# Reordered first loads and a tile of ones for the junk products, in a linear-attention and MLP-mixer kernel

## The chip, the cores and the metric

The kernel runs on one core of a Trainium2 chip. The core has five engines, each with its own instruction queue: TensorE (PE, matrix products; its weight loads are shown as PEld), VectorE (DVE), ScalarE (ACT), GpSimd (POOL) and SyncE (SP), which issues most of the transfers between device memory and on-chip memory. Sixteen transfer engines (DMA) carry them; loads that SP issues go into one set of queues, those that ACT issues into another. The metric is the device time of one execution in microseconds (us); less is better. Before the change it is 771.73 us, the median of three runs (771.15 to 772.42).

## The reference

Two blocks follow one another, in float32, with batch 8, 8 heads, 576 tokens and head size 64 (8 x 64 = 512 channels):

```python
kv  = einsum('bhsd,bhse->bhde', k, v)          # per head 64 x 64, summed over the 576 tokens
out = einsum('bhsd,bhde->bhse', q, kv)
x   = out / sqrt(mean(out * out, -1) + 1e-6) * g_norm   # then heads side by side: 576 x 512 per batch
h   = relu(x.T @ w_tok1) @ w_tok2              # 576 -> 256 -> 576, over tokens
u   = x + h.T
out = u + relu(u @ w_ch1) @ w_ch2              # 512 -> 1536 -> 512, over channels
```

The weights of the second block arrive as 64-bit floats and are turned into 32-bit ones on the chip.

## The kernel before

The batch is worked on in pairs. For each pair the attention runs first, then the mixing over tokens, and, after all pairs, the mixing over channels, which takes about two thirds of the time. The change touches only the first microseconds.

Of each batch's 576 tokens the first 512 are loaded as four rows of products (J = 4), the last 64 as a fifth. `load(b)` (line 141) brings k and v of batch b: for each a large transfer of 1 MB into `k_in[:, :4]` or `v_in[:, :4]`, and two small ones of 64 KB each, 32 token rows apiece, into the fifth row (j = 4). The other half of the fifth row's 128 partitions is zeroed by POOL (line 1286). For batch 0, k goes through SP's queue and v through ACT's; for later batches everything goes through SP's. `load_q(b)` (line 152) brings the transposed q (1 MB for 512 tokens). `get_tok1` (line 216) fetches the first token weights as raw 64-bit words into `raw`; ACT and DVE then turn them into `w_tok1` in four steps (lines 166 to 190).

The order in which the first loads are written is: `load(0)` (k, v and their small loads), `load_q(0)`, two blocks of `w_tok1`, `load(1)`, `load_q(1)`, the 64 last tokens of q for both batches, the last block of `w_tok1`; later in the text comes `g_norm` (`g_row`, one row of 256 bytes, on ACT's queue). Each engine keeps this order of its own instructions.

The order of the computing work is written out by hand as a list of short names, `start` (line 1304). Its first line begins with `j12`: `keep_warm(12)` (line 1341), twelve products of the identity with itself, whose result nobody reads. Then `kv00` and `kv01`, the products of k and v of batch 0 (`ps_kv`, 80 passes; a float32 product is two passes), each followed by `e00`, `e01`, a copy to `kvp`; `gs`, `spread_g` (line 1298), which spreads `g_row` to all 128 partitions by a product with a row of ones (`ps_g`) and a copy to `g_sb`; then `a00` to `a11`, the products with q (`ps_o`, 8 passes each); on DVE and ACT the factor g, the squares, their sums and the scaling; the steps `w01` to `w04`, the conversion of the first token weights; `j8`, eight more junk products; and `h000`, `h010`, the first products with them (`ps_h`). `kv10` is the `ps_kv` of batch 1.

For `kv00`, the products of j = 0 to 3 of the first half of the columns come first and need only the large loads; the next one, j = 4, reads the fifth row and so needs all four small loads:

```python
for i in range(2):
    for j in range(JJ):
        for h in range(2):
            matmul(o[...], lhsT=kk[:, j, at], rhs=vv[:, j, at], start=(j == 0), stop=(j == JJ - 1))
```

The semaphores between engines and transfers are set by the compiler layer. In the trace each load that SP or ACT issues takes one of eight counters in turn, and a load whose counter is still in use waits for the load that has it.

## Time and profile before

| what | value |
| --- | --- |
| median of the runs | 771.73 us |
| the profiled execution, time / span | 771.12 / 769.3 us |
| granted clock of PE | 0.999 |
| PE busy | 759.4 us, 99% of the span |
| DVE, ACT, POOL busy | 642.5, 277.4, 112.3 us |
| first junk product on PE | 3.34 us |
| first `ps_kv` product, and the restart after a wait | 8.81 and 9.82 us |
| first `ps_o` | 12.19 us |
| `ps_kv` of batch 1 | 21.67 us |

The span runs from the first instruction to the last; the execution's time has 1.8 us more around it. The profile lists groups of instructions with an engine, a line of the code, the tile that is written and those that are read. "Busy" is the time in which an engine worked on such instructions; behind it stand the idle time before a group and what ended that idle time. In the table of windows the columns are the stretch, its length, busy time and instructions of PE, PEld, DVE, ACT and POOL, the granted clock, the mean busy share of the transfer engines, and GB/s. `w_tok<-raw`, `x<-ps_o,g_sb` and the like read "written from".

### The profile page before, as it was taken

To read this page: it belongs to the slowest core of one execution; us is meant where nothing else is said; L and a number is where in the kernel's file an instruction comes from. 1 tells how busy PE (TensorE), PEld (TensorE's weight loads), DVE (VectorE), ACT (ScalarE), POOL (GpSimd) and SP (SyncE) were. 2 spreads that over 40 slices of the span, in tenths; PEclk is the share of its full clock that TensorE was granted. 3 is DMA by queue.
4 is the path that set the end of the run, shared out by engine and by line. 5 is a ranking of instruction groups with operands and counts; after the bars stand their busy time and mean duration, and the time that the engine had idled before them with its cause. 6 is when DMAs were issued, how large, how long until landed. Compare 5 with 4: busy or idle time off the path is not lost.

```text
span 769.3 us, 12678 instructions
## 1 busy us (share of the span) xinstructions
PE 759.4 (99%) x4676; PEld 612.3 (80%) x4676; DVE 642.5 (84%) x945; ACT 277.4 (36%) x556; POOL 112.3 (15%) x125
## 2 busy tenths in 40 slices
PE   7999999999999999999999999999999999999998
PEld 6665555445888888888888888888888888888887
DVE  3868897997767779899969889987998996798996
ACT  3555575764210233511244242123352223325221
POOL 1003020213410000002240001042000218000204
PEclk9999999999999999999999999999999999999999
DMA  9999998499699786589998577999659879955679
GB/s 339 366 366 370 373 372 301 151 318 342 251 286 339 271 282 191 164 270 207 216 236 251 158 224 216 255 188 267 202 148 290 172 220 208 207 145 157 151 200 119
DMA packets 137677, 188.26 MB, mean 245 GB/s; under 512 B 48658, under 2 KB 95250, under 8 KB 135570
## 3 DMA queue, kind: packets, MB, share of 16 engines
q1 hardware_dynamic: 101744, 167.54, 68.9%
q0 software_dynamic: 34816, 18.36, 16.1%
q10 hardware_dynamic: 1058, 1.57, 0.6%
q8 instruction: 37, 0.61, 0.3%
q14 instruction: 22, 0.18, 0.1%
HBM read 138.28 MB, written 49.15 MB: 244 GB/s over the span
## 4 chain that ended last, share of the span: by engine, by line
PE 97%; DMA 2%; SPq 0%; issue 0%; DVE 0%
PE ps_d L136 28%; PE ps_b L136 19%; PE ps_a L136 19%; PE ps_u L136 8%; PE ps_h L136 8%; PE ps_v L136 5%; PE ps_c L136 3%; DMA v_in<-in_v_dram 2%; PE ps_kv L136 2%; PE ps_o L136 2%; PE ps_w L136 2%; SPq L124 0%; PE ps_r L136 0%; DVE xs L127 0%
## 5 line engine op out<-in xcount | busy, mean ns | idle before, releaser
L136 PE MATMUL ps_d<-ui,w 128*128 128x256 f32 x504 | 118.6, 379 | 0.0
L136 PEld LDWEIGHTS ps_d<-ui,w 128*128 128x128 f32 x504 | 95.9, 190 | 12.9
L133 ACT COPY ps_d<-ps_a 128x768 f32<-128x768 f32 (+1 forms) x56 | 32.0, 572 | 200.2 <-PE ps_a L136 197.2
L127 DVE TENSOR_TENSOR v<-v,v 128x1536 f32<-128x1536 f32 (+2 forms) x70 | 103.2, 1482 | 0.3
L136 PE MATMUL ps_b<-sv,w 128*128 128x256 f32 x324 | 78.9, 380 | 0.0
L136 PE MATMUL ps_a<-v,w 128*128 128x256 f32 x324 | 78.8, 379 | 0.0
L1206 POOL DMA_DIRECT2D out_dram<-us x24 | 26.7, 1833 | 291.8 <-ACT p L133 286.2
L136 PEld LDWEIGHTS ps_b<-sv,w 128*128 128x128 f32 x324 | 61.3, 190 | 8.8 <-issue 0.6
L136 PEld LDWEIGHTS ps_a<-v,w 128*128 128x128 f32 x324 | 61.7, 190 | 8.2
L136 PE MATMUL ps_u<-h,w_tok 128*128 128x512 f32 (+1 forms) x160 | 64.7, 599 | 0.0
L136 PE MATMUL ps_d<-v,w 128*128 128x256 f32 x258 | 62.7, 379 | 0.0
L130 ACT ACTIVATE v<-v 128x768 f32<-128x768 f32 (+1 forms) x54 | 42.6, 822 | 55.1 <-DVE v L127 52.3
L136 PE MATMUL ps_h<-x,w_tok 128*128 128x512 f32 x128 | 57.8, 600 | 0.7 <-DVE w_tok L190 0.7
L1206 POOL DMA_DIRECT2D out_dram<-r x40 | 41.3, 1927 | 102.0 <-ACT p L133 80.3
L136 PE MATMUL ps_d<-sv,w 128*128 128x256 f32 x228 | 55.4, 379 | 0.0
L136 PEld LDWEIGHTS ps_d<-v,w 128*128 128x128 f32 x258 | 49.0, 190 | 6.5
L136 PEld LDWEIGHTS ps_u<-h,w_tok 128*128 128x128 f32 (+1 forms) x160 | 25.6, 179 | 31.1 <-issue 26.7
L136 PEld LDWEIGHTS ps_d<-sv,w 128*128 128x128 f32 x228 | 43.4, 190 | 5.8
L136 PE MATMUL ps_a<-uT,w 128*128 128x256 f32 x192 | 46.7, 379 | 0.0
L136 PEld LDWEIGHTS ps_h<-x,w_tok 128*128 128x128 f32 x128 | 23.4, 190 | 27.1 <-issue 24.1
L136 PE MATMUL ps_b<-ui,w 128*128 128x256 f32 x168 | 40.8, 379 | 0.0
L136 PEld LDWEIGHTS ps_a<-uT,w 128*128 128x128 f32 x192 | 36.5, 190 | 4.9
(169 smaller groups left out, 1288.0 us busy)
## 6 DMA issues: line engine op xcount, KB each, us to landing
w<-parts SPq DMA_DIRECT2D x168, 384.0 KB
w<-parts SPq DMA_DIRECT2D x56, 192.0 KB
uT<-blocks SPq DMA_DIRECT2D x36, 256.0 KB
k_in<-in_k_dram SPq DMA_DIRECT2D x8, 1024.0 KB
qT<-in_q_dram SPq DMA_DIRECT2D x8, 1024.0 KB
out_dram<-x POOLq DMA_DIRECT2D x16, 512.0 KB, 7.0
v_in<-in_v_dram SPq DMA_DIRECT2D x7, 1024.0 KB
raw<-in_moe_w_ch_dram SPq DMA_DIRECT2D x8, 768.0 KB
```

Source lines behind the costliest of these rows:

```text
L127: keep(engine.tensor_tensor(out=o, in0=a, in1=b, op=op))
L130: keep(nc.scalar.activation(o, a, AF.Relu))
L133: keep(nc.scalar.copy(o, a))
L136: keep(nc.tensor.matmul(*a, **kw))
L1206: keep(nc.gpsimd.dma_start(to, t()[ds(b * Q, Q), at].rearrange("p n l j -> p n (l j)"), accum_op=ALU.add))
```

## The change

The change has three parts. In `load(0)`, k's and v's large loads are issued as before (SP and ACT), then q of batch 0 on SP's queue, and then all four small loads on ACT's queue; later batches load as before. The text of the load of g is as it was, and comes later on ACT's queue. The junk products now multiply a 128 x 128 tile of ones, which DVE writes ahead of its other clears; the identity, which POOL made, is gone, and so is POOL's row of ones: `spread_g` uses the first row of the tile. The first row of junk products has 16 instead of 12.

```diff
-    ident = inp.tile([P, P], F32, name="ident")
+    ones = inp.tile([P, P], F32, name="ones")
-    g_row, ones = (inp.tile([1, n], F32, name=name) for n, name in ((D, "g_row"), (P, "ones")))
+    g_row = inp.tile([1, D], F32, name="g_row")
...
-        queues = (nc.sync, nc.sync if b else nc.scalar)
-        for dst, t, e in zip((k_in[b % 2], v_in[b % 2]), (k, v), queues):
-            dma(dst[:, :J], t[b, :LO].rearrange("(p j) e -> p j e", j=J), e)
+        both = ((k_in[b % 2], k), (v_in[b % 2], v))
+
+        def rest(dst, t, queue):
             for n in range(0, HF, Q):
-                dma(dst[n:n + Q, J], t[b, LO + n:LO + n + Q].rearrange("(r e) d -> e r d", e=8), e)
+                dma(dst[n:n + Q, J], t[b, LO + n:LO + n + Q].rearrange("(r e) d -> e r d", e=8), queue)
+
+        for dst, t in both:
+            dma(dst[:, :J], t[b, :LO].rearrange("(p j) e -> p j e", j=J), nc.sync if b or t is k else nc.scalar)
+            if b:
+                rest(dst, t, nc.sync)
+        if b == 0:
+            load_q(0)
+            for dst, t in both:
+                rest(dst, t, nc.scalar)
...
     load(0)
-    load_q(0)
...
+    keep(nc.vector.memset(ones, 1.0))
     for t in zeroed:
         keep(nc.vector.memset(t, 0.0))
...
-    make_identity(nc, ident)
-    keep(nc.gpsimd.memset(ones, 1.0))
...
-        matmul(o[:, :D], lhsT=ones, rhs=g_row, start=True, stop=True)
+        matmul(o[:, :D], lhsT=ones[:1], rhs=g_row, start=True, stop=True)
...
-        "j12 kv00 e00", "kv01 gs e01 l0", "a00 g00 q00", "a01 g01 q01 t00 t01 m0 w01",
+        "j16 kv00 e00", "kv01 gs e01 l0", "a00 g00 q00", "a01 g01 q01 t00 t01 m0 w01",
...
-            matmul(o[:, :P], lhsT=ident, rhs=ident, start=True, stop=True)
-
-    more |= {f"j{n}": do(keep_warm, n) for n in (8, 12)}
+            matmul(o[:, :P], lhsT=ones, rhs=ones, start=True, stop=True)
+
+    more |= {f"j{n}": do(keep_warm, n) for n in (8, 16)}
```

More of the change, by code (lines that the diff above doesn't have):

```diff
@@ L9 @@
 from concourse.dve_ops import ADD32_U16LIMBS
-from concourse.masks import make_identity
 F32 = mybir.dt.float32
```

## The prediction

> **What bounds the kernel now.** I read four views in this order: the clock, the busy table, the chain that ended last, and, since the change lies in the first 20 us, the waits and the time line there.

> ```profile
> core 0: 769.3 us, clock 0.999
> PE 759.4 (99%) x4676; PEld 612.3 (80%) x4676; DVE 642.5 (84%) x945; ACT 277.4 (36%) x556; POOL 112.3 (15%) x125
> PE 97%; DMA 2%; SPq 0%; issue 0%; DVE 0%
> ```

> The clock is full and TensorE (PE) is the bound: it is idle for 769.3 - 759.4 = 9.9 us, and the time line puts 3.7 us of that behind the last product (from 765.5 on). The other 6.1 us lie before 21.67 us, and no wait of PE is recorded after that. So whatever moves the product at 21.67 us moves the end by as much, and nothing behind it gives time back. The chain in its first part, with start, length and what:

> ```profile
> 0.75 7.97 DMA v_in<-in_v_dram
> ...
> 11.65 9.89 DMA v_in<-in_v_dram
> 21.54 0.14 issue
> 21.67 2.55 PE ps_kv L136 x80
> ```

> The gate at 21.67 is the landing of the second batch's v. How near is PE's own work to being the gate? The same stretch on PE (start, length, line, count, idle before it and what ended it):

> ```profile
> 8.81 0.69 PE L136 MATMUL ps_kv<-v_in,k_in 128*64 128x64 f32 x16 [0.85 <-DMA v_in<-in_v_dram]
> 9.82 2.09 PE L136 MATMUL ps_kv<-v_in,k_in 128*64 128x64 f32 x64 [0.32 <-DMA v_in<-in_v_dram]
> 11.83 0.43 PE L136 MATMUL ps_g<-g_row,ones 1*128 1x64 f32 x2
> 12.19 2.05 PE L136 MATMUL ps_o<-kvp,qT 128*128 128x128 f32 x16
> ```

> The first 16 products need the large loads of k and v (j = 0 to 3); then PE waits for the remainder rows (j = 4), which all four small loads bring. From 12.19 a dense chain runs (products, squares on ACT, reductions and the first token weights on DVE) up to the `ps_h` products at 19.35, whose four passes end at 21.33. Then come 0.34 us of idleness, put down to the second v. So **PE's chain has 0.34 us of slack against the transfers**: a chain that is d late costs d - 0.34, and a chain that is early gains nothing unless that v lands earlier too. Can it? The busy share of the transfer engines and GB/s (last two columns):

> ```profile
> 3.34:7.96 4.62, 4.62 (x24) 4.43 (x24) 0.00 (x0) 1.37 (x2) 0.09 (x1) 1.00 0.97 401
> 9.82:11.91 2.09, 2.09 (x65) 2.02 (x65) 0.42 (x1) 0.00 (x0) 0.00 (x0) 1.00 0.99 321
> 11.91:14.24 2.33, 2.33 (x18) 2.08 (x18) 1.12 (x2) 0.27 (x2) 0.00 (x0) 1.00 1.05 338
> 14.83:18.67 3.84, 3.84 (x32) 3.65 (x32) 3.63 (x12) 3.61 (x10) 0.00 (x0) 1.00 1.00 411
> ```

> They are full from 3.3 us on. The change moves the same bytes ahead of that v, on the same engines, so I leave its landing at 21.5.

> **The change part by part.**

> *Junk products.* POOL's identity (0.21 + 0.29 us) and its row of ones (0.19) go; DVE writes a 128x128 tile of ones before its two PSUM clears (0.27 each). DVE starts at 0.88, so the tile is there at about 1.1 and PE starts at 1.2 rather than 3.34. DVE's next work is at 10.77, so the extra 0.2 us there costs nothing. Twelve junk products are 24 passes, sixteen are 32. In the window view 15 passes started within 3.35 us (about 213 ns apart) and then the rest at about 111 ns, so the first 3.4 us were slow. Repeating this from 1.2: 16 slow passes to 4.6, 16 fast ones to 6.4; if all stay slow, 32 x 213 = 6.8 us, to 8.0. Both end before the large loads land (8.7). Cost: nothing, covered by the wait for k and v; but PE's idle stretch before 8.81 grows from 0.85 us to between 0.8 and 2.4.

> *q behind k.* On SP's queue q is now second rather than fourth. That q is not late today: its first reader starts at 12.19, 0.28 us after `ps_kv` ends at 11.91, with `ps_g` in between. Gain at most 0.1 us, taken as zero.

> *The four remainder loads.* Each is 64 KB. k's two went on SP's queue ahead of q, v's two on ACT's; now all four are on ACT's queue behind v, while q's megabyte streams on SP's. Issuing them costs ACT four times about 0.7 us (row of three: 2.44 us) and pushes its table load (1.28 us) from 3.2 to about 5; ACT's next work is at 12.30, so that is covered. Landing is not. Today the queues run in step: from the landing of the large loads (first products at 8.81) to the restart at 9.82 are 1.01 us, in which each queue carries two small loads. With four in one queue beside q's stream in the other they get the same share but twice the bytes. Bounds: zero, if they have priority; 0.26 MB at 400 GB/s is 0.65 us if they shared nothing; a doubling of two loads' stay gives 1.0; and 16 passes of 2 KB per engine at 84 ns (the packets' records), each alternating with one of q, are 1.35 us more than today. I take 1.35, since the records of landings show the four loads arriving in turns of 0.65 us, k's and v's alternating (8.71, 8.92, 9.37, 9.57). So PE restarts at **11.15**, and `ps_kv` ends 2.09 us later at 13.24.

> [...]

> *g.* Its 256-byte load is today issued at 3.30 and is needed at 11.83. SP's queue shows that loads wait for earlier ones: SP stands still until 8.74 on v, then issues the ninth load. Eight loads go out, and each next one waits for the one eight places before it. With ACT's five loads ahead of g and SP free to issue the token weights early, g falls behind these eight and waits for one of them. Which one the trace can't show. If for k, v or a small load (8.7 to 9.6), g is there by 11.5 and costs nothing. If for q (landed 12.02), it is issued at 12.0; issue to first packet took 0.8 us for the first k, last packet to landing 0.6, so it lands at 13.5 or somewhat later behind traffic; I take 13.75. PE's order puts `ps_g` ahead of the first `ps_o`: 13.75 + 0.36 = **14.1** instead of 12.19. The bounds are no extra and, if it waited for the first token weights (in use at 15.5), 3 us. I take q, being third or fourth in the order of issue. On ACT only g's copy stands behind that wait, and PE stands behind that copy's product. The last small load may have to wait for v as well (8.54); issued then, it reaches its queue before the others are through.

> *Other queues.* SP issues the first token weights earlier by up to 6 us, behind q in the same queue; they are used at 15.50, when ACT gets to them, so an early landing gains nothing. POOL loses 0.7 us of work that nobody else waits for.

> **Sum.** `ps_o` starts 14.1 - 12.19 = 1.9 us late; the chain to 21.33 follows one for one (ACT and DVE are each busy 3.6 of 3.84 us there); slack 0.34 goes off: +1.57 us. The profiled execution took 771.12 (769.3 and 1.8 around it), 0.6 below the median. Put on the median, 771.73 + 1.57 = **773.3**, +0.2%, which is just about what a measurement of this kernel can tell from no change.

> **The rivals.**

> *g in time (A).* Only the small loads are late: 13.24 + 0.36 + small waits puts `ps_o` at 13.5, 1.35 late: 1.35 - 0.34 = +1.0, **772.7**. It wins if g waits for one that lands by 10.

> *PE turns slow again (B).* Between the junk's end (6.4) and 11.15 PE has 0.69 us of work in 4.75 us; today it never idles over 0.85 us in that time and stays fast. If it falls back, 64 passes of `ps_kv` at twice 29 ns cost 1.9 us more, and some of `ps_o` up to 16 x 0.1 = 1.6: +1.9 to +3.5 on top of +1.0 or +1.6, so **775.0** in the middle. For it: the first junk passes were slow for 3.4 us. Against: the j8 products ran fast after gaps of 0.6. [...]

> *Not slower: small loads unharmed (C).* If the small loads keep their pace, arriving up to 0.34 us late and g in time, the slack swallows it: **771.7**. It decides where the restart comes before 10.2. For it: 0.13 MB more in one queue is only 0.33 us at 400 GB/s. Against: the alternating landings.

> *Faster stream (D).* If q beside v rather than beside token weights lifts the 321 to 338 GB/s between 9.8 and 14.2 to 410, the second v lands 0.8 us earlier, and filling the first 3.3 us (share 0.47) could give up to 1 us more. PE's chain must shorten too: up to 1.8 us, **769.9**. Nothing shows q's place as the cause.

> **How the numbers follow.** Rests and g late 0.40 (773.3, from 772.9 to 773.9); A 0.20; B 0.24 (773.9 to 776); C 0.09; D 0.07. Range: from 771.3 (leaves out D and some of C) to 775.4 (leaves out the upper part of B). Slower by over 0.2% (above 773.27): B and some 0.27 of the first case, 0.51. Faster by over 0.2%: 0.06, D at its full size. Same: 0.43.

> **What would show it.** The first 16 `ps_kv` passes stay at 8.8; the wait behind them grows from 0.32 us to 1.5 or more; `ps_g` waits for its load; the wait at 21.67 for v vanishes and the second `ps_kv` starts at about 23.2. `ps_kv` at 58 ns a pass means B. A second `ps_kv` still gated by v before 21.7 means C or D. The prediction is wrong if the last small load lands by 10, or if g waits for more than q.

## The result and the profile after

The changed kernel takes 774.19 us in the median of nine runs (772.10 to 775.28), the kernel before 771.15 beside it. The ratio is 1.0035, with a 95% interval of 1.0024 to 1.0046: slower by about a third of a percent, 3.0 us. The forecast was 773.3 us, with a range of 771.3 to 775.4.

The profiled execution took 775.23 us. Its span and granted clock:

```profile
core 0: 773.1 us, clock 0.996
```

Its busy table:

```profile
PE 763.9 (99%) x4684; PEld 616.0 (80%) x4684; DVE 642.8 (83%) x946; ACT 277.5 (36%) x556; POOL 111.7 (14%) x122
```

PE's busy time has grown by 4.5 us, though only eight passes were added; no other engine's has grown by more than 0.3 us. The chain that ended last, from 3.9 us on (start, length, what):

```profile
3.92 7.56 DMA v_in<-in_v_dram
11.48 0.14 issue
11.61 2.79 PE ps_kv L135 x64
14.41 0.61 PE ps_g L135 x2
15.02 3.73 PE ps_o L135 x16
...
23.85 1.98 PE ps_h L135 x4
25.83 2.48 PE ps_kv L135 x80
```

The chain no longer goes through the second batch's v. It starts from the last small load of batch 0, which ACT issued at 3.92 and which lands at 11.48; from there it is PE's own chain up to the second batch's products. The same stretch on PE's time line:

```profile
1.07 6.12 PE L135 MATMUL ps_j<-ones 128*128 128x128 f32 x32 [1.07 <-DVE ones L1295]
8.73 0.69 PE L135 MATMUL ps_kv<-v_in,k_in 128*64 128x64 f32 x16 [1.53 <-DMA v_in<-in_v_dram]
11.61 2.79 PE L135 MATMUL ps_kv<-v_in,k_in 128*64 128x64 f32 x64 [2.20 <-DMA v_in<-in_v_dram]
14.34 0.69 PE L135 MATMUL ps_g<-g_row,ones 1*128 1x64 f32 x2
14.95 6.35 PE L135 MATMUL ps_o<-kvp,qT 128*128 128x128 f32 x32
23.85 1.98 PE L135 MATMUL ps_h<-x,w_tok 128*128 128x512 f32 x4 [0.76 <-DVE w_tok L198]
```

The large loads are as early as before (8.73 against 8.81). The wait for the small ones has grown from 0.32 to 2.20 us. Then the same 64 passes take 2.79 us instead of 2.09, and the products with q are stretched too. The windows say why; the columns after PE, PEld, DVE, ACT and POOL are the granted clock, the transfer engines' share and GB/s:

```profile
5.90:9.31 3.41, 1.88 (x28) 1.68 (x26) 0.00 (x0) 0.22 (x2) 0.00 (x0) 1.00 1.00 405
9.31:12.72 3.41, 1.21 (x42) 1.14 (x39) 0.15 (x1) 0.00 (x0) 0.00 (x0) 1.00 1.05 386
12.72:16.14 3.42, 3.42 (x41) 3.19 (x37) 0.70 (x2) 0.21 (x1) 0.00 (x0) 0.50 1.06 404
16.14:19.55 3.41, 3.41 (x18) 3.34 (x17) 1.47 (x3) 0.65 (x2) 0.00 (x0) 0.50 0.91 350
```

From 12.72 to 19.55 us the granted clock is one half. This is rival B. In the profiled execution the delay against the kernel before grows like this:

| point of the program | before | after | late by |
| --- | --- | --- | --- |
| products of k and v restart | 9.82 | 11.61 | 1.79 |
| first `ps_o` | 12.19 | 14.95 | 2.76 |
| first `ps_h` | 19.35 | 23.85 | 4.50 |
| second batch's `ps_kv` | 21.67 | 25.76 | 4.09 |
| `ps_h` of four passes after it | 28.12 | 32.01 | 3.89 |
| span | 769.3 | 773.1 | 3.8 |

From 28 us on the delay stays within 0.1 us of that to the end. This was the second slowest of the nine runs. Two of the nine, with a clock of 1.000, had spans of 770.0 and 770.1; the other seven, with 0.996 to 0.998, 771.5 to 773.1. The time outside the span was 1.8 us before; now it lies between 2.1 and 3.7, 2.7 in the median. So there are three sums to explain: late loads, a clock that falls in most runs, and 0.9 us outside the span that no step of the prediction named.

### The profile page after: what moved, and what is told of

It reads as the page before. It is cut to its first block, busy times and chain, and to the rows that moved or that the text cites. A ratio compares the mean times of both kernels' runs of the same rounds, so it can differ in the third digit from the quotient of the medians.

```text
span 773.1 us, 12692 instructions
## 1 busy us (share of the span) xinstructions
PE 763.9 (99%) x4684; PEld 616.0 (80%) x4684; DVE 642.8 (83%) x946; ACT 277.5 (36%) x556; POOL 111.7 (14%) x122
## 4 chain that ended last, share of the span: by engine, by line
PE 97%; DMA 1%; DVE 1%; ACTq 0%; issue 0%; ACT 0%
PE ps_d L135 28%; PE ps_b L135 19%; PE ps_a L135 19%; PE ps_h L135 8%; PE ps_u L135 8%; PE ps_v L135 5%; PE ps_c L135 3%; PE ps_o L135 3%; PE ps_kv L135 3%; PE ps_w L135 2%; DMA v_in<-in_v_dram 1%; ACTq L123 0%; PE ps_r L135 0%; DVE x L461 0%; DVE ms L482 0%
```

## The experiments

The theory after the result: the small loads come late because they share with q's stream, PE idles, and the clock falls. The rivals: the junk products alone carry the loss, or the loads do without the clock.

### Only the loads

```diff
--- before
...
+        for dst, t in both:
+            dma(dst[:, :J], ..., nc.sync if b or t is k else nc.scalar)
...
+        if b == 0:
+            load_q(0)
+            for dst, t in both:
+                rest(dst, t, nc.scalar)
...
     load(0)
-    load_q(0)
```

`load` is the whole of the changed kernel's `load`; a line of three points stands for lines left out, here and below.

> Only the loads are reordered; the junk products stay twelve products of the identity, from 3.3 to 8.0 us. Theory (late small loads, and then the clock of TensorE falls back in the longer idle time): the products of k and v restart at about 11.5 us instead of 9.8, which alone is 1.8 - 0.34 = +1.4 us at most; with the junk ending only 0.8 us before the large loads land, the clock falls back more seldom than in the changed kernel, so +1 to +3 us over the kernel before, 772 to 774. Rival (the earlier junk products, or the tile of ones, carry the loss): no change, 771.2, and a clock of 1.000 in every run.

Measured: 773.39 us against 771.88 (12 and 33 runs), ratio 1.0012 (1.0003 to 1.0020). Spans are 771.4 to 771.8 in the eight runs with a clock of 0.998 and 770.1 to 770.7 in the four with 1.000. PE's time line in the profiled execution:

```profile
3.35 4.81 PE L136 MATMUL ps_j<-ident 128*128 128x128 f32 x24 [3.35 <-POOL ident masks.py:199]
11.38 3.31 PE L136 MATMUL ps_kv<-v_in,k_in 128*64 128x64 f32 x64 [1.87 <-DMA v_in<-in_v_dram]
```

and the window in which its clock (third number from the end) is halved:

```profile
10.70:14.12 3.42, 2.74 (x52) 2.77 (x54) 0.42 (x1) 0.00 (x0) 0.00 (x0) 0.50 1.07 402
```

The loads alone bring the late restart and, in eight of twelve runs, the clock's fall, even with the junk ending at 8.16. I had expected the fall to be rarer than in the changed kernel (seven of nine); it hardly is. The two rivals that put everything on the junk, or on the clock being a bystander, do not stand: within this one kernel the halved clock goes with about 1.4 us more span (medians 771.6 and 770.2).

### Only the junk products

```diff
--- after
...
-        if b == 0:
-            load_q(0)
-            for dst, t in both:
-                rest(dst, t, nc.scalar)
...
     load(0)
+    load_q(0)
```

`load` is again that of the kernel before.

> Only the junk products change (tile of ones by VectorE, sixteen instead of twelve, from 1.1 us); the loads are as before. Theory: the restart stays at 9.8 us and the idle time before it is 1.5 + 0.3 us with 0.7 us of work between, so the clock stays full in most runs: 771.2, at most +0.5. Rival (the junk carries the loss): +2 to +3, and the clock falls to half behind 12 us.

Measured: 772.40 us, ratio 1.0004 (0.9994 to 1.0014), not to be told from no change. The spans are even a little shorter, 769.5 in the median against 770.1; but the time outside them is 1.8 to 3.6 us, 2.4 in the median, against 1.73 to 1.86 in all 33 runs of the kernel before. One of the twelve runs has a clock of 0.998; none of the 33 of the kernel before has less than 0.999.

### The small loads in sixteen parts

```diff
--- after
+            e = 8 if b else 16
...
-                dma(dst[n:n + Q, J], t[...].rearrange("(r e) d -> e r d", e=8), queue)
+                dma(dst[n:n + Q, J], t[...].rearrange("(r e) d -> e r d", e=e), queue)
```

> The changed kernel with the four small loads of batch 0 spread with a slowest dimension of 16 instead of 8. Theory (all four pile up on the same eight transfer engines, beside q's stream): twice the engines halve the pile, the last small load lands by about 10.0 us instead of 11.5, the products restart at 10.2, and the clock falls back seldom: 771.5 to 772.3. Rival (they are late because their queue gets half of all bandwidth, or because of the order of issue): landing stays at 11 us or later, 774.

Measured: 774.43 us, ratio 1.0034 (1.0022 to 1.0046): no better than the change. The records of landings give 9.17, 9.74, 10.32 and 10.87 us for the four, against 9.19, 9.96, 10.72 and 11.48 in the changed kernel. The products restart at 11.00 instead of 11.61:

```profile
11.00 3.26 PE L135 MATMUL ps_kv<-v_in,k_in 128*64 128x64 f32 x64 [1.38 <-DMA v_in<-in_v_dram]
```

In the three other profiled executions with this order and eight parts the last small load landed at 11.06 to 11.24 and the products restarted at 11.21 to 11.38. Sixteen parts instead of eight are thus worth 0.2 to 0.6 us at the restart, not most of the delay; that a pile on eight engines causes that delay was not shown. The clock still falls (0.998 or less in seven of ten runs). The spans are 771.25 in the median against 771.6; the time outside them is longer, 3.34 us.

### TensorE kept busy

```diff
--- after
+                    if whole and side == half == i == 0 and j == J:
+                        keep_warm(9)
...
-        "j16 kv00 e00", ...
+        "j22 kv00 e00", ...
...
```

> The changed kernel with 22 junk products at the start instead of 16, and nine more in the wait between the large and the small loads, so that TensorE is never idle for long before 11.6 us. Theory that the clock's fall to half costs about two thirds of the loss: restart still at 11.6, passes of 29 ns and a clock of 1.000 in all runs, spans alike from run to run, +0.8 to +1.4 us over the kernel before: 772.0 to 772.6. Rival (the late loads alone carry the loss, the clock is a bystander): 774 as with the change.

Measured: 772.70 us (772.38 to 773.10, the narrowest of all), ratio 1.0008 (1.0000 to 1.0017). Spans are 770.3 to 771.0, and the clock is 0.999 or 1.000 in all twelve runs. Time line:

```profile
9.00 2.27 PE L135 MATMUL ps_j<-ones 128*128 128x128 f32 x18
11.21 2.09 PE L135 MATMUL ps_kv<-v_in,k_in 128*64 128x64 f32 x64
13.22 0.43 PE L135 MATMUL ps_g<-g_row,ones 1*128 1x64 f32 x2
22.67 2.55 PE L135 MATMUL ps_kv<-v_in,k_in 128*64 128x64 f32 x80
```

With more work, and loads nearly as late (the last small one lands at 11.06), the kernel is faster. The 64 passes are back at 2.09 us. The second `ps_kv` starts 1.00 us late (22.67 against 21.67) after a restart 1.39 late, 0.34 having gone into the slack: this is the cost of the late loads alone, and the prediction's rival A in size. The changed kernel's spans are 1.0 us longer (771.6 in the median against 770.6 here); what differs between the two is the clock, though they were not measured beside each other.

### All small loads ahead of q

Here the second row of junk has four products instead of eight, so that PE's program is as long as before the change; why that matters is the subject of the next part.

```diff
--- after
-            load_q(0)
             for dst, t in both:
-                rest(dst, t, nc.scalar)
+                rest(dst, t, nc.sync)
+            load_q(0)
```

> The changed kernel (with four in the second junk row) with all four small loads on SyncE's queue ahead of q, so that they share with v's tail only and not with q's stream. Theory (they are late because each alternates with packets of q): last landing at about 9.6 to 9.9, restart of the products at 9.9 to 10.2, no long idle time and no fall of the clock in most runs, a span near 769.5 to 770 and 771.3 to 772. Rival (four in one queue are late wherever they stand): restart at 11 or later, span 771.5, 773.4.

Measured: 772.01 us against 771.30 (11 and 31 runs), ratio 1.0007 (0.9998 to 1.0017), not to be told from no change; clock 0.999 or 1.000 in all runs. The last small load lands at 9.33 us, and PE waits for it by 0.06 us at most:

```profile
8.72 2.83 PE L135 MATMUL ps_kv<-v_in,k_in 128*64 128x64 f32 x80 [1.80 <-DMA v_in<-in_v_dram]
12.13 2.02 PE L135 MATMUL ps_o<-kvp,qT 128*128 128x128 f32 x16 [0.21 <-DVE kvp L399]
21.66 2.55 PE L135 MATMUL ps_kv<-v_in,k_in 128*64 128x64 f32 x73 [0.44 <-DMA v_in<-in_v_dram]
26.08 1.13 PE L135 MATMUL ps_o<-kvp,qT 128*128 128x128 f32 x8 [0.60 <-DVE x L519]
```

Four in one queue are not late in themselves (9.33 us); on ACT's queue, beside q's stream, the last one landed at 11.06 to 11.48. Nor is it the time of issue: here the last one is issued at 3.60 us, in the changed kernel at 3.92. The queue and the place ahead of q were changed together, so which of the two it takes was not separated. The run also shows that an early start of the products gains nothing: the first `ps_o` waits for q (landed 11.99; the copy that the profile names is the second one to `kvp`, and the first products read only what the first copy wrote), and the second `ps_kv` starts at 21.66, when the second v lands, as before. The last line shows a gate behind it that I had not seen. The wait is put down to DVE by the profile, but the second q lands at 25.95 in the records, and the first product that reads it starts at 26.08. In the kernel before it landed at 25.10, and that product started at 25.24, before the DVE work of that kind ended there (26.13). So this execution lost 0.84 us there though it was on time at 21.66. That landing lies between 24.2 and 26.0 in the ten profiled executions, and may be part of why the kernel before spreads over 3 us at full clock; this was not tested by itself.

### PE's program as long as before

```diff
--- the kernel with only the junk changed / the changed kernel
...
-        ... w11 j8", ...
+        ... w11 j4", ...
...
```

> The loads as before, junk from the tile of ones as in the change, but the second row of junk has four products instead of eight, so that TensorE's program is as long as before the change. In the run with the junk alone the time outside the span was between 1.8 and 3.6 us (median 2.4), with the kernel before always 1.8. Theory (the 16 more instructions on TensorE make the end of its program need one more block of instructions, which is fetched after the span): 1.8 in all runs here, the span as with the junk alone, 769.5 in the median, so 771.3, 0.5 us faster than the kernel before. Rival (the time outside comes from the tile of ones or VectorE's write): 1.8 to 3.6 again, 772.4.

> The changed kernel with four instead of eight products in the second row of junk, so that TensorE's program is as long as before the change. Theory: the time outside the span is 1.8 to 1.9 in all runs instead of 2.1 to 3.7, the span stays at 771.6 in the median with the clock's fall in most runs, so 773.4: the changed kernel loses 0.8 to 0.9 us less. Rival: 774.2 as with the change.

And the other way round, the kernel before with sixteen instructions more:

```diff
--- before
...
-        "j12 kv00 e00", ...
+        "j16 kv00 e00", ...
...
```

> The kernel before with 16 instead of 12 products of the identity in the first row, nothing else. Theory: the time outside the span becomes 2 to 3.5 us in some or all runs, since TensorE's program grows by 16 instructions, though loads and identity are as before; the span stays at 769.3 to 770.1 (the junk ends at 8.9 instead of 8.0, at the landing of the large loads): 771.9 to 773. Rival: 1.8 outside and 771.9 or less.

The first was expected half a microsecond ahead of the kernel before and is level with it (771.11 against 771.30; its clock falls in some of the eleven runs, to 0.998 in two). The second took 772.97 us, with a median span of 770.9 rather than 771.6, since its clock fell in four of nine runs; its time outside the span was expected at 1.8 to 1.9 and is 2.1. The third took 772.15 us; its junk lasted until 10.1 us instead of the expected 8.9 and held the first products back until 10.06. The times outside the span, which these runs were for, with those of the other kernels beside them:

| kernel | PE junk | ratio to before | time outside the span: least, median, most |
| --- | --- | --- | --- |
| before (31 runs) | 12 + 8 | 1 | 1.74, 1.79, 1.87 |
| changed kernel | 16 + 8 | 1.0035 | 2.09, 2.69, 3.69 |
| changed, small loads in sixteen parts | 16 + 8 | 1.0034 | 2.06, 3.34, 3.66 |
| changed, program as long as before | 16 + 4 | 1.0023 (1.0011 to 1.0035) | 2.07, 2.12, 2.18 |
| changed, small loads ahead of q | 16 + 4 | 1.0007 | 2.06, 2.08, 2.17 |
| changed, TensorE kept busy | 22 + 9 + 8 | 1.0008 | 2.06, 2.10, 2.14 |
| only loads | 12 + 8 | 1.0012 | 1.85, 1.87, 1.94 |
| only junk | 16 + 8 | 1.0004 | 1.77, 2.42, 3.56 |
| only junk, program as long as before | 16 + 4 | 1.0005 (0.9996 to 1.0013) | 1.80, 1.84, 1.90 |
| before with 16 | 16 + 8 | 1.0010 (1.0001 to 1.0018) | 1.81, 1.94, 2.96 |

The tails of 2.5 us and more appear with 16 + 8, with either tile and either order of the loads, and vanish with 16 + 4. So they go with the number of PE's instructions, not with the tile of ones. The record of one such run supports the reason that I gave: in the kernel with the loads in sixteen parts (16 + 8, 3.4 us outside) the profile holds 38 fetches of 16 KB on the instruction queue, the last at 773.3 us, 2.3 us behind the end of its span; before, there are 37, the last at 748.4. With still more products (22 + 9 + 8, the kernel kept busy) the 38th fetch comes at 763.1, in time, and the time outside is 2.1 in every run. The other three profiled executions with 16 + 8 had short tails (1.9 to 2.1 us) and hold 37 fetches. So the late fetch goes with the long tail; that the end waits for it, and why the same program has it in some executions only, was not shown. The 0.3 us that stay in the changed kernel with its program as long as before are not explained either: the least time outside the span is 2.06 to 2.09 in every kernel that has both the tile of ones and other loads than before, and 1.77 to 1.85 in those with only one of the two.

## Why the prediction was right, and where it was wrong

**Right in time and sign.** 774.19 lies in the range and 0.9 us above the forecast; 3.0 us (0.35%) above the median of the nine runs of before. The three steps that carried it did not fare alike.

**The small loads.** "I take 1.35 ... PE restarts at 11.15." It restarted at 11.61 in the profiled execution, and at 11.2 to 11.4 in three others with this order. The four landed 0.76 us apart (9.19 to 11.48), where my estimate of turns taken packet by packet, four of the load's and four of q's of 84 ns on each of eight engines, would give 0.67; and putting them ahead of q took the delay away (last landing 9.33). So q's stream was right as the place to look, and the term was 0.1 to 0.5 us too small at the restart. Turns packet by packet are not shown: in sixteen parts the same sum would give 0.34, and they landed 0.57 apart.

The sixteen passes per engine in that term come from the eight landings that each small load shows in the records (a large one shows sixteen), taken as eight engines: 256 KB in packets of 2 KB. That is my estimate, and it weighed too much: in sixteen parts the four still took until 10.87, 0.2 to 0.6 us less, where half of the 1.35 would be 0.67. The 8.54 us that the prediction takes for v is k's landing (v's is 8.72), and the last small load waited for neither: it was issued at 3.92.

**The likeliest case fell: g.** "I take q, being third or fourth in the order of issue." ACT issued g at 8.66, when v had landed, not at 12.0. It landed at 13.44 even so, close to my 13.75, but not for my reason: its one packet moved at 12.83, 1.35 us after the last small load had landed, and the records don't show what it stood behind. (The 0.8 us in that sum, from issue to first packet, is 1.03 in the records: 0.75 to 1.78.) And PE ended `ps_kv` at 14.4 there and didn't wait for it. In the kernel kept busy it landed at 13.02, and `ps_g` started at 13.22 without a wait. So the step "14.1 instead of 12.19" is to be struck out; with a clock that stays full, `ps_o` started at 13.58, as rival A had it (13.5). A's loss of 1.0 us is what that kernel shows at its second `ps_kv`; its ratio gives 0.6 us (0 to 1.3).

**Rival B happened.** It had 0.24; the clock fell in seven of nine runs of the changed kernel. Its price, +1.9 to +3.5, was too high for most runs: 64 passes of `ps_kv` and part of `ps_o` cost 1.5 us of span in most runs (771.5 to 771.6 against 770.0 to 770.1) and 2.7 in the profiled one, where the halved stretch was twice as long as in the four other profiled executions with a fall, 6.83 us against 3.41 (0.97 more at `ps_o`'s start, 1.74 more from there to `ps_h`). What I held against B, that the j8 products ran fast after gaps of 0.6 us, said nothing about what came: two gaps of 1.53 and 2.20 us with 0.69 us of work between them.

**The slack.** "Nothing behind it gives time back" was wrong by 0.2 us: 4.09 late at the second `ps_kv` became 3.89 at 28 us, since before the change the second q (landed 25.10) held PE at 25.24 for a moment that the matmuls' modelled ends hide. The landing of the second v was left at 21.5. It was 21.74 in the changed kernel and 21.47 with the small loads in sixteen parts, but 20.41 to 20.59 in the three other profiled executions with this order: the 0.8 us and more that rival D hoped for, and worth nothing, since PE's chain came later than that in each of them.

**Missed.** The 0.9 us outside the span. I had costed four more junk products at nothing, "covered by the wait for k and v". Their execution is covered; their place in the program is not.

So the sum, corrected for medians: late loads +0.7 (a span of 770.0 to 770.1 in the two runs at full clock, against 771.15 - 1.79 = 769.4 before), the clock +1.5 in seven of nine runs, outside the span +0.9: 3.1, measured 3.0. That the forecast was near it is partly luck: a wrong 0.6 for g stood where the clock and the tail belonged.

## What to carry to other kernels

A load that is small and needed soon should stand ahead of a large one in the same stream: ahead of q the last of 256 KB landed at 9.33 us (queue and place changed together), while on another queue beside q it came 1.5 to 1.9 us later than before the change (11.06 to 11.48 us against 9.57). Before paying for an idle gap on TensorE at face value, add up its work over the few microseconds around the gap, since here a wait of 2 us (2.20 in the profiled execution) was followed by a halved clock, which cost another 1.5 in most runs. Added instructions that cost nothing where they ran went with more time behind the last one (sixteen on PE: 1.8 us outside the span became 1.8 to 3.6); look at the time outside the span.

## What the runs showed of the hardware that I had not expected

Fall: the change with an equally long program, the change, sixteen parts, only junk with equally long program, only loads.

```profile
8.02:11.43 3.41, 0.81 (x20) 0.74 (x22) 0.00 (x0) 0.00 (x0) 0.00 (x0) 1.00 1.05 397
```

```profile
6.81:10.22 3.41, 1.51 (x23) 1.21 (x22) 0.00 (x0) 0.00 (x0) 0.00 (x0) 1.00 1.04 335
```

```profile
6.75:10.17 3.42, 1.54 (x24) 1.25 (x23) 0.00 (x0) 0.00 (x0) 0.00 (x0) 1.00 1.01 398
```

```profile
7.29:10.70 3.41, 1.55 (x24) 1.25 (x22) 0.00 (x0) 0.00 (x0) 0.00 (x0) 1.00 1.01 387
```

(The change itself is the window 9.31:12.72 shown above, 1.21.) No fall: small loads ahead of q, only junk, before.

```profile
5.32:8.73 3.41, 1.60 (x15) 1.44 (x15) 0.00 (x0) 0.00 (x0) 0.00 (x0) 1.00 0.99 405
```

```profile
6.36:9.77 3.41, 1.74 (x25) 1.44 (x24) 0.00 (x0) 0.00 (x0) 0.00 (x0) 1.00 1.00 399
```

```profile
6.88:10.30 3.42, 2.25 (x42) 1.98 (x42) 0.00 (x0) 0.00 (x0) 0.00 (x0) 1.00 1.01 396
```

The fourth without a fall is the window 5.90:9.31 of the change, 1.88. With 1.55 us of work or less the clock was halved for the next stretch, with 1.60 or more it was not: the border in these executions lies at about 46% of 3.41 us. The end of the span fits in: in the run with only the junk the stretch 764.12:767.53 had 1.64 us and no fall behind it, in the kernel before 764.64:768.05 had 0.91 and the clock was halved from 768.05. The longest gap does not sort them. With only the junk and an equally long program the clock fell behind gaps of 1.20 and 0.69 us, while it stayed full behind the 1.80 us shown above for the small loads ahead of q:

```profile
8.81 0.69 PE L135 MATMUL ps_kv<-v_in,k_in 128*64 128x64 f32 x16 [1.20 <-DMA v_in<-in_v_dram]
10.19 3.61 PE L135 MATMUL ps_kv<-v_in,k_in 128*64 128x64 f32 x64 [0.69 <-DMA v_in<-in_v_dram]
```

The stretches are few, the busy time counts modelled ends, and the weight loads' time sorts them as well, so the border is an observation. One stretch goes against it: in the change PE was busy for the whole of 12.72:16.14, at half clock, and the next stretch was halved too, while in the four other executions with a fall the clock came back after one. What ends a fall was not found. The edges lie at another place in each run (4.6 to 9.6 us for the first full clock), which is probably why the same program falls in one run and not in the next; only one execution of each has a trace.
